# Constant products in TensorE's gaps at the handovers between the layers of a recurrent attention kernel

## The chip, the cores and the metric

The kernel runs on one core of a Trainium2 chip. The time is the device time of the core in microseconds; the number that counts is the median of several executions. A profile is one execution, recorded instruction by instruction by the hardware profiler.

## The reference, cut to what matters

Two kinds of layer alternate, A, B, A, B, each added to its input behind a layernorm. The input has 2048 tokens of width 512.

```python
# A: 64 segments of 32 tokens, one after the other, with 8 memory rows ahead of each
for s in range(n_seg):
    h = jnp.concatenate([mem, xs], axis=1)          # 40 rows
    q = jnp.einsum('btd,dhe->bhte', h, Wq)          # 32 heads of 128; k and v alike
    ...
    o = jnp.einsum('bhqk,bhke->bhqe', p, v)         # p: masked softmax
    o = jnp.einsum('bhte,hed->btd', o, Wo)
    mem = o[:, :M, :]                               # the next segment's memory
# B: linear attention over all tokens
kv = jnp.einsum('bhsd,bhse->bhde', pk, v)           # sums over every token
z = jnp.einsum('bhsd->bhd', pk)
o = num / den                                       # num = pq kv, den = pq z
x = x + o @ wo
```

Two things are serial by nature. A segment of A needs the memory rows of the segment before it. A token of B needs `kv` and `z` of all tokens, so no row of B can be finished before the last segment of A has run, and the second A can't start before the first tile of B is finished.

## The kernel before, in words

Weights stay in SBUF. The tokens are cut into 16 tiles of 128 rows (`NT`), a tile into four segments; `a_layer` loops over the 64 segments (`NSEG`). For a segment, the projections at L794 multiply the 40 rows by Wk, Wq and Wv (four products side by side in the array, each 32 columns wide). The results go through a transpose (L816, L842, or a DMA), scores (L937, L943), softmax, values (L980, L983, L1051), and then the output projection at L1085. The segment's output comes as two halves that L1110 (for the memory) or L1121 (for the tokens) adds up. The work of B is spread between the segments: `b_in` takes a finished tile of A through a layernorm (L753 to L759, transposed at L765), computes its keys and values (L1247), and adds the tile's part to `kva` (L1274) and `za` (L1276). `b_out` takes a tile back from DRAM as the second A layer needs it.

The handover from A through B to the next A is a single chain, for which no other work is left. In order:

- the last segment's output projection, L1085, its two copies on ScalarE (L623), and L1146, a product that puts the rows of the last segment into a tile; L1150 adds them to `x_sb`
- the layernorm of that last tile: L753, L754 on VectorE, L755, L757 on ScalarE, L759 on VectorE, the transpose L765 and its copy (L624)
- `b_in` of the last tile: keys and values by L1247 (4 products of 512 columns each), the function phi of the keys (L1231 on ScalarE, L1232 and L1234 on VectorE), the value copy (L623), `z` (L1265), `kv` (L1259), the queries (L1281), and the sums L1276 and L1274
- `b_mid`: the mask over the finished sums (L1295, L1299) and four products with the output weights, L1303, each copied back
- `b_out` of the first tile: L1350, its reciprocal as Ln and Exp on ScalarE (L1353, L1355), L1356, L1358 (4 products), and L1361, which adds the result to `x_sb`
- the layernorm of that tile for the second A layer, L753 to L765, the copies into `hT`, and the first projections, L794

After the second A and its `b_mid`, `b_out` runs over all 16 tiles instead, with nothing behind it; the tiles' inputs are loaded in large transfers by `last_rows`, while the last segments run.

The order of the work is not written out by hand. Each operation is a node of `_Prog` with its reads, writes, PSUM tiles and a cost from small formulas (`c_act`, `c_dve`, `c_pe`). `schedule` plays the engines in the planner's own time and picks, for each free engine, the ready node with the highest `prio`. A node's `prio` is the negative of its due time: `step * PERIOD + OFFSET[name][k]`, from a table with an entry for the k-th node of each named place. Nothing is picked ahead of a more urgent node that comes ready within `LOOK` (0.053 us). `finalize` then turns the edges (`sync`) into semaphore waits; an `order` edge only fixes the order on one engine. On the chip each engine runs its list in that order, whatever is ready behind. A PSUM tile is given one of 8 banks when its first node is placed.

One place already uses constant products: `warm` (L733 to L742) puts 14 products of `id_sb` and `Wq_sb` (L740) into the first segment, after its second scores.

Of the kernel before, what the change touches and what calls it, by code (L numbers as in the profile page):

```python
# [47 lines left out]
    "mem0F": (-317.25, -11.55, -397.30, -321.65, -320.25, -248.15, -253.70, -229.35, -133.00, -179.30),  # L48
    "mem1F": (-370.65, -140.65, -279.95, -318.75, -212.15, -221.80, -405.65, -341.75, -281.65, -211.10),
    "warm": (42.25,),  # L50
    "outF": (-402.35, -81.30, -402.15, -242.85, -347.15, -401.55, -307.80, -298.10, -276.25, -259.15),
    "nextF": (-375.70, -276.25, -244.45),
    "xF": (-98.95, -278.35, -377.95, -152.15, -135.25, 32.50, -346.60, -281.05, -333.80, -305.40, -12.30, -315.60,
# [49 lines left out]
def c_act(n, ptr=0, sb=0):  # L103
    return 0.17 + 0.833e-3 * n + 0.09 * ptr + 0.04 * sb


def c_dve(n, rate=1):
    return 0.155 + 1.044e-3 * n / rate
# [6 lines left out]
def c_pe(n_mm, n):  # L115
    return n_mm * max(0.0335, (n / 2.4 + 3.0) * 1e-3)
# [24 lines left out]
class _Prog:  # L141
# [27 lines left out]
    def add(self, engs, fn, cost, reads=(), writes=(), tiles=(), dsem=None, urgent=False, mode="full",  # L169
            after=(), lat=0.0):  # L170
        nd = _Node()
        nd.mode = mode
        nd.lat = lat
        nd.key = None
        if self.place is not None:
            step, name = self.place
            nd.key = (step, name, self.count)
            self.count += 1
        nd.soft = set()
        nd.engs = (engs,) if isinstance(engs, str) else tuple(engs)  # L180
        nd.cost = cost if isinstance(cost, dict) else {e: cost for e in nd.engs}
        nd.fn = fn
        nd.sync = set(after)
        nd.order = set()
        nd.tiles = tuple(tiles)
        nd.dsem = dsem
        nd.urgent = urgent
        nd.eng = nd.start = nd.done = nd.know = None
        nd.sig = False
        nd.val = 0  # L190
        nd.waits = []
        nd.idx = len(self.nodes)
        if dsem is not None:
            self.dma_tot[dsem] = self.dma_tot.get(dsem, 0) + 16
            nd.dval = self.dma_tot[dsem]
        for key in reads:
            st = self.res.setdefault(key, [None, []])
            if st[0] is not None:
                nd.sync.add(st[0])
            st[1].append(nd)  # L200
        for key in writes:
            st = self.res.setdefault(key, [None, []])
            if st[0] is not None and st[0] is not nd:
                nd.sync.add(st[0])
            for r in st[1]:
                if r is not nd:
                    nd.sync.add(r)
            st[0] = nd
            st[1] = []
        for tl in nd.tiles:  # L210
            if tl.ops:
                p = tl.ops[-1]
                if p.engs == ("pe",) and nd.engs == ("pe",):
                    nd.order.add(p)
                else:
                    nd.sync.add(p)
            tl.ops.append(nd)
        self.nodes.append(nd)
        return nd
# [270 lines left out]
def bass_interleave_layers__memory_aug_recurrent_mem_tr__linear_attn_block__prompt_kernel(  # L490
    nc: bass.Bass,
    A_x: bass.AP,
    A_mem0: bass.AP,
    A_Wq: bass.AP,
    A_Wk: bass.AP,
    A_Wv: bass.AP,
    A_Wo: bass.AP,
    A_seg_len: bass.AP,
    B_x: bass.AP,
    B_wqkv: bass.AP,  # L500
    B_wo: bass.AP,
    out: bass.AP,
):
    _build_kernel(nc, A_x, A_mem0, A_Wq, A_Wk, A_Wv, A_Wo, A_seg_len, B_wqkv, B_wo, out)


def _build_kernel(nc, A_x, A_mem0, A_Wq, A_Wk, A_Wv, A_Wo, A_seg_len, B_wqkv, B_wo, out):
# [8 lines left out]
    NSEG = S // SEG  # L516
# [14 lines left out]
    def sb(name, shape, dt=BF16):  # L531
        return E(nc.sbuf_tensor(name, shape, dt))
# [3 lines left out]
    Wv_sb = sb("Wv_sb", [128, 4, H * DH])  # L536
# [3 lines left out]
    id_sb = sb("id_sb", [128, 128])  # L540
# [76 lines left out]
    P = _Prog(nc, banks)  # L617
    add = P.add
# [19 lines left out]
    def x_move(o, i, k, reads, writes, kind, eng="pool", lat=2.0):  # L638
        add(eng, lambda e: e.dma_start(o, i), 0.55 if eng == "pool" else 0.4, reads=reads, writes=writes,  # L639
            dsem="%s%d" % (kind, k), lat=lat + (0.4 if eng == "pool" else 0.0))  # L640
# [3 lines left out]
    def slot(t):  # L644

        return (t + shift[0]) % NX
# [20 lines left out]
    def load_wo_b(n):  # L667
        add("pool", lambda e: e.dma_start(MB_sb[:, :, :], B_wo.rearrange("(c p) f -> p c f", p=128)), 1.1, after=[late[-1]],
            writes=[("MB", c) for c in range(4)], dsem="dwoB%d" % n, lat=4.0)
# [33 lines left out]
    for j in range(4):  # L703
# [15 lines left out]
    tl = P.tile()  # L719
    add("pe", lambda t, tl=tl: t.matmul(tl.f32()[:, 0:128], A8_sb[0:8, :], A8_sb[0:8, :], start=True, stop=True), 0.06,  # L720
        reads=XV, tiles=[tl])
    evac(maskbd_sb[:, :], lambda tl=tl: tl.f32()[:, 0:128], 128, tiles=[tl], writes=["maskbd"])
    tl = P.tile()
# [604 lines left out]
    def b_out(step, t, last):  # L1328

        P.at(step, ("boL" if t < NT - 1 else "boZ") if last else "bo" if t else "boF")  # L1330
        k = slot(t)
        x, xk = x_sb[:, k, :], ("x", k)
        e, ek, rb, rk = OWN if t else LEFT
        free = []
        if last:
            rb, rk = RE[:, t, :].bitcast(F32), [("RE", t)]
            free = P.res["Wk"][1]
            if t < NT - 1:
                e, ek, x, xk = XE[:, 0, t, :], [("XE", 0, t)], XE[:, 1, t, :], ("XE", 1, t)
            else:  # L1340
                e, ek = e_sb, ["e"]
        else:
            x_move(x, xs_view[t], k, [("xs", t)], [xk], "dxl")
            x_move(e, pq_view[t], k, [("pq", t)], ek, "dql" if t else "dq0")
        td, ty = P.tile(), P.tile()

        def md(pe):
            for c in range(4):
                o = slice(128 * c, 128 * c + 128)
                y = pe.matmul(td.f32()[:, o], zf_sb[:, c, :], e[:, o], start=True, stop=True)  # L1350
            return y
        add("pe", md, c_pe(4, 128), reads=["zf"] + ek, tiles=[td])
        add("act", lambda a: a.activation(rb, td.f32()[:, :], ACTF.Ln, bias=eps6_sb[:, 0:1]), c_act(512, 1),  # L1353
            reads=["eps6"], tiles=[td], writes=rk, after=free)
        add("act", lambda a: a.activation(rb, rb, ACTF.Exp, scale=-1.0), c_act(512, 0, 1), reads=rk, writes=rk)  # L1355
        add("dve", lambda v: v.tensor_tensor(e, e, rb, ALU.mult), c_dve(512), reads=ek + rk, writes=ek)  # L1356
        for c in range(4):
            add("pe", lambda pe, c=c: pe.matmul(ty.f32()[:, :], e[:, 128 * c:128 * c + 128], MB_sb[:, c, :],  # L1358
                                                start=(c == 0), stop=(c == 3)),
                c_pe(1, 512), reads=ek + [("MB", i) for i in range(4)], tiles=[ty])  # L1360
        add("dve", lambda v: v.tensor_tensor(x, x, ty.f32()[:, :], ALU.add), c_dve(512), reads=[xk], writes=[xk],  # L1361
            tiles=[ty])
        if last:
            x_move(o_view[t], x, t % 4, [xk], [], "dout", "sp")

    load_wo_b(1)
    a_layer(0, True)
    b_mid(NSEG + 2, 1)
# [5 lines left out]
    b_mid(2 * NSEG + 2, 3)  # L1374
    for t in range(NT):
        b_out(2 * NSEG + 2 + t, t, True)
    P.schedule()

    with nc.Block() as blk:
# [40 lines left out]
```

## Time and profile before

| | |
|---|---|
| Median of 5 runs | 1786.98 us (1782.03 to 1799.78) |
| The profiled execution: its own time | 1789.46 us |
| its span, from the first to the last instruction | 1787.3 us |
| TensorE busy in the span | 1665.1 us, 43,964 products |
| VectorE, ScalarE busy | 1061.6 us, 1172.0 us |
| Mean granted TensorE clock | 0.988 |
| PE busy in a stage inside the first layer (200 to 300 us) | 95.8 us of 100, clock 1.00 |
| PE busy in 870 to 880, 880 to 890, 890 to 900 us | 5.4, 5.5, 8.7 us of 10; clock 0.84, 0.84, 0.63 |
| PE busy in 1740 to 1750, 1750 to 1760 us | 7.4, 5.2 us of 10; clock 0.69, 0.67 |

The profile is read so: a row of the timeline gives the start, the time from the first start to the last end of a group of equal instructions, the engine, line and operation, and in brackets the idle time ahead of it with what ended it. The granted clock is a share of TensorE's full clock. The end of a product is modelled, about 0.2 us after its last column is issued, so that rows that follow each other overlap.

### The profile page before, as it was taken

The page shows a single profiled execution, that of the slowest core. Times are in us where ns is not written, and L with a number is a line of the kernel's source. Part 1 is how long each engine was busy: PE and PEld are TensorE (multiplying, and loading weights), DVE is VectorE, ACT ScalarE, POOL GpSimd, SP SyncE. Part 2 cuts the span into 40 slices and gives each one's busy share as a digit, 9 for nine tenths or more (in the row PEclk, how much of TensorE's full clock was granted, in tenths as well). Part 3 has the DMA queues.
Part 4 walks back from the last instruction along what each step waited for, and adds up shares of the span by engine and source line. Part 5 has one row for each costly group of instructions (what it writes and reads, how often), then busy time and mean ns, then how long its engine had stood idle before and what let it go on. Part 6 is the DMA issues. An engine that isn't in the chain of part 4 may idle for free.

```text
span 1787.3 us, 96722 instructions
## 1 busy us (share of the span) xinstructions
PE 1665.1 (93%) x43964; PEld 1068.6 (60%) x44043; DVE 1061.6 (59%) x3788; ACT 1172.0 (66%) x3117; POOL 326.3 (18%) x660
## 2 busy tenths in 40 slices
PE   5999999999999999999799999999999999999997
PEld 2656666665666665566455566656656656666563
DVE  3456666665666565565555566656655656665656
ACT  3666666666666666666466676767666766676665
POOL 2011212111221211222102111122211112221120
PEclk9999999999999999999899999999999999999998
DMA  9222323323233332332012333233333332332333
GB/s 377 78 48 53 57 53 53 58 51 56 50 57 53 54 58 47 56 56 51 21 34 44 56 56 64 46 59 59 55 57 56 52 57 53 59 57 53 61 77 98
DMA packets 295978, 113.46 MB, mean 63 GB/s; under 512 B 274552, under 2 KB 289712, under 8 KB 294032
## 3 DMA queue, kind: packets, MB, share of 16 engines
q1 hardware_dynamic: 272240, 74.91, 23.7%
q0 software_dynamic: 21744, 19.78, 5.4%
q10 hardware_dynamic: 1584, 12.58, 1.7%
q8 instruction: 344, 5.64, 1.4%
q14 instruction: 66, 0.54, 0.1%
HBM read 29.63 MB, written 10.49 MB: 22 GB/s over the span
## 4 chain that ended last, share of the span: by engine, by line
PE 63%; DMA 20%; DVE 9%; ACT 5%; issue 2%; POOL 1%; ACTq 0%; DVEq 0%
PE pb L794 31%; DMA arena_sb<-arena_sb 14%; PE pb L1085 12%; PE pb L1051 3%; PE pb L1247 3%; DVE arena_sb L624 3%; DMA dx_sb<-y_sb 2%; PE pb L816 2%; PE pb L970 2%; DMA arena_sb<-pq_scratch 2%; PE pb L937 1%; DMA Wk_sb<-in_A_Wk_dram 1%; ACT arena_sb L623 1%; PE pb L1281 1%; PE pb L1019 1%
## 5 line engine op out<-in xcount | busy, mean ns | idle before, releaser
L623 ACT ACTIVATE arena_sb<-pb 128x512 bf16<-128x512 f32 (+6 forms) x1433 | 709.7, 500 | 296.2 <-PE pb L794 187.2
L639 POOL DMA_DIRECT2D dx_sb<-y_sb x504 | 253.6, 509 | 1129.8 <-DVE arena_sb L624 659.5
L794 PE MATMUL pb<-Wv_sb,arena_sb 128*32 128x512 bf16 x5120 | 357.3, 379 | 2.6 <-issue 2.6
L794 PE MATMUL pb<-Wq_sb,arena_sb 128*32 128x512 bf16 x5120 | 347.4, 382 | 0.9 <-DMA Wq_sb<-in_A_Wq_dram 0.6
L1085 PE MATMUL pb<-Wo_sb,arena_sb 128*32 128x256 bf16 x10368 | 341.7, 276 | 6.8 <-DVE arena_sb L987 5.1
L794 PE MATMUL pb<-Wk_sb,arena_sb 128*32 128x512 bf16 x5120 | 343.9, 382 | 4.3 <-DMA Wk_sb<-in_A_Wk_dram 2.9
L1085 PEld LDWEIGHTS pb<-Wo_sb,arena_sb 128*32 128x32 bf16 x10368 | 264.6, 98 | 48.8 <-DVE arena_sb L987 12.9
L624 DVE COPY arena_sb<-arena_sb 128x128 bf16<-128x128 bf16 (+2 forms) x973 | 207.5, 213 | 143.4 <-DMA arena_sb<-arena_sb 89.0
L624 DVE COPY arena_sb<-pb 128x512 bf16<-128x512 bf16 (+2 forms) x311 | 117.9, 381 | 198.5 <-PE pb L816 177.6
L624 DVE CAST arena_sb<-pb 128x512 bf16<-128x512 f32 (+3 forms) x388 | 186.9, 488 | 43.6 <-PE pb L794 27.8
L794 PEld LDWEIGHTS pb<-Wk_sb,arena_sb 128*32 128x32 bf16 x5120 | 127.2, 97 | 129.5 <-DVE arena_sb L624 19.1
L794 PEld LDWEIGHTS pb<-Wq_sb,arena_sb 128*32 128x32 bf16 x5120 | 135.2, 98 | 115.4 <-issue 3.7
L623 ACT ACTIVATE outW_sb<-pb 128x128 fp32r<-128x128 f32 x290 | 80.3, 277 | 108.2 <-PE pb L1085 98.5
L794 PEld LDWEIGHTS pb<-Wv_sb,arena_sb 128*32 128x32 bf16 x5120 | 113.1, 95 | 59.2 <-issue 4.2
L954 ACT ACTIVATE arena_sb<-pb 128x192 bf16<-128x192 f32 (+1 forms) x256 | 84.0, 328 | 85.8 <-PE pb L937 84.1
L964 DVE TENSOR_TENSOR arena_sb<-arena_sb 128x128 bf16<-128x128 bf16 x504 | 90.6, 221 | 26.3 <-ACT arena_sb L954 22.3
L816 PEld LDWEIGHTS pb<-id_sb,arena_sb 128*32 128x32 bf16 x4320 | 82.1, 97 | 32.2 <-issue 1.4
L1051 PE MATMUL pb<-arena_sb 128*128 128x128 bf16 x1024 | 98.7, 221 | 1.5 <-DVE arena_sb L624 0.5
L816 PE MATMUL pb<-id_sb,arena_sb 128*32 128x128 bf16 x4320 | 97.1, 220 | 0.7 <-ACT arena_sb L623 0.7
L987 DVE TENSOR_TENSOR arena_sb<-pb,arena_sb 128x128 bf16<-128x128 f32 x252 | 68.8, 287 | 43.2 <-ACT arena_sb L975 31.2
L937 PE MATMUL pb<-arena_sb 128*32 128x40 bf16 x4096 | 69.1, 180 | 27.0 <-DMA arena_sb<-arena_sb 26.6
L1121 DVE TENSOR_TENSOR y_sb<-pb,outW_sb 64x256 bf16<-64x256 f32 x158 | 65.7, 416 | 44.3 <-ACT outW_sb L623 40.4
(122 smaller groups left out, 1966.9 us busy)
## 6 DMA issues: line engine op xcount, KB each, us to landing
arena_sb<-arena_sb SPq DMA_TRANSPOSE x480, 2.8
Wq_sb<-in_A_Wq_dram ACTq DMA_DIRECT2D x1, 4096.0 KB, 13.6
Wk_sb<-in_A_Wk_dram ACTq DMA_DIRECT2D x1, 4096.0 KB, 24.4
Wv_sb<-in_A_Wv_dram ACTq DMA_DIRECT2D x1, 4096.0 KB, 34.8
Wo_sb<-in_A_Wo_dram SPq DMA_DIRECT2D x4, 1024.0 KB, 11.7
xs_scratch<-x_sb POOLq DMA_DIRECT2D x32, 128.0 KB, 2.2
pq_scratch<-arena_sb POOLq DMA_DIRECT2D x32, 128.0 KB, 2.2
dx_sb<-y_sb POOLq DMA_DIRECT2D x252, 12.0 KB
```

What stands on the lines that cost most here:

```text
L623: return e.activation(o() if callable(o) else o, i() if callable(i) else i, ACTF.Copy)
L624: return e.tensor_copy(o() if callable(o) else o, i() if callable(i) else i)
L639: add(eng, lambda e: e.dma_start(o, i), 0.55 if eng == "pool" else 0.4, reads=reads, writes=writes, dsem="%s%d" % (kind, k), lat=lat + (0. ...
L794: r = pe.matmul(tl.f32()[32 * j:32 * j + 32, 0:512], blk[:, c, :], W[:, c, o:o + 512], start=(c == 0), stop=(c == 3), tile_position=(0, 32 ...
L816: r = pe.transpose(tt.bf16()[32 * j:32 * j + 32, 128 * i:128 * i + 128], img[:, k, o:o + 32], id_sb[:, :], tile_position=(0, 32 * j))
L937: r = pe.matmul(tl.f32()[32 * j:32 * j + 32, 40 * i:40 * i + 40], kT[:, hh, j, :], qT[:, hh, j, :], start=True, stop=True, tile_position=( ...
L954: add("act", lambda a: a.activation(PQ[:, r2, b, 0:nq], tl.f32()[:, 0:nq], ACTF.Exp, scale=SCALE), c_act(nq), tiles=[tl], writes=[("PQ", r ...
L964: add("dve", lambda v, a=a, p_=p_, w_=w_: v.tensor_tensor(wide(Pm[:, k, a, :]), p_.unsqueeze(2).to_broadcast([128, 4, 4, 8]), w_, ALU.mult ...
L987: add("dve", lambda v: v.tensor_tensor(oTb[:, s % NO, 16 * b:16 * b + 16, 0:8], pv.f32()[:, 0:128].rearrange("p (n q) -> p n q", q=8), Rm[ ...
L1051: r = pe.matmul(o, vimg[:, r2, e], Pbx[:, hh, :, :], start=i == 0, stop=False, skip_group_check=True)
L1085: r = pe.matmul(tl.f32()[32 * j:32 * j + 32, 0:256], oT[:, 4 * hh + n, :], Wo_sb[:, 8 * n + hh, 256 * d:256 * d + 256], start=(hh == 0 and ...
L1121: add("dve", lambda v: v.tensor_tensor(y_sb[0:64, k, :], tl.f32()[0:64, 0:256], outW[64:128, w, :].bitcast(F32), ALU.add), c_dve(256), rea ...
```

## The change

A function `keep_busy` is called after everything else has been put down and before `schedule`. It adds products of `id_sb` (128 x 128) and the first 256 columns of `Wv_sb` in 8 places; each place has one PSUM tile, which nobody reads. A place is tied by an `order` edge to one node of the chain, after which its products may stand, and the table gives all of them a due time 200 us behind their step, later than that of other work.

```diff
     "warm": (42.25,),
+    "fill": (200.00,),
...
+    FILL = (("outL", 7, 12), ("resL", 0, 24), ("biL", 5, 4), ("biL", 18, 8), ("biL", 27, 8), ("bm", 7, 21), ("boF", 9, 22),
+            ("prepF", 5, 4))
+
+    def keep_busy():
+
+        last = {n.key: n for n in P.nodes if n.engs == ("pe",) and n.key is not None}
+        for base in (0, NSEG):
+            for name, k, n in FILL:
+                step = base + NSEG + {"outL": 0, "resL": 0, "boF": -6, "prepF": -2}.get(name, 2)
+                node = last.get((step, name, k))
+                if node is None or (base and name == "bm"):
+                    continue
+                P.at(step, "fill")
+                tl = P.tile()
+                for i in range(n):
+                    P.count = 0
+                    nd = add("pe", lambda pe, tl=tl: pe.matmul(tl.f32()[:, 0:256], id_sb[:, :], Wv_sb[:, 0, 0:256], start=True,
+                                                               stop=True),
+                             c_pe(1, 256), reads=["id", "Wv"], tiles=[tl])
+                    if i == 0:
+                        nd.order.add(node)
+
...
         b_out(2 * NSEG + 2 + t, t, True)
+    keep_busy()
     P.schedule()
```

The third number of each entry is how many products stand at that place: 12 behind the last L1085, 24 behind L1146, 4 behind the transposes L765 of the last tile, 8 behind the values of L1247, 8 behind the queries L1281, 21 behind the second product of L1303, 22 behind the first tile's L1358, and 4 behind the transposes L765 of the next layer. As the planner places them, the 21 stand behind all four of L1303 and behind L1350. The first handover has all eight places (103 products). The second has the first five (56): the names of the last two don't occur there, and `bm` is left out by hand.

## Prediction

> **What bounds the kernel now.** I read the page first: its row of slices and its chain. Then I asked for the PE timeline around the two places where a layer pair ends, for the chain of waits there, and for stages of 1 us.
>
> ```profile
> PE   5999999999999999999799999999999999999997
> ...
> PEclk9999999999999999999899999999999999999998
> ...
> PE 63%; DMA 20%; DVE 9%; ACT 5%; issue 2%; POOL 1%; ACTq 0%; DVEq 0%
> ```
>
> TensorE is busy 93% of the span and carries 63% of the chain, so for most of the time the kernel is bound by products at full clock. Slices 20 and 40 are the exceptions: PE falls to 7 tenths and the clock to 8. These are the two handovers that the change touches. The PE timeline of the first one:
>
> ```profile
> 870.28 1.93 PE L1085 MATMUL pb<-Wo_sb,arena_sb 128*32 128x256 bf16 x64 [0.27 <-ACT arena_sb L623]
> 872.90 0.50 PE L1146 MATMUL pb<-outW_sb,selz_sb 128*128 128x256 f32 x2 [0.69 <-ACT outW_sb L623]
> 876.14 0.40 PE L765 MATMUL pb<-id_sb,arena_sb 128*128 128x128 bf16 x4 [2.74 <-DVE arena_sb L759]
> 877.46 3.05 PE L1247 MATMUL pb<-arena_sb 128*128 128x512 bf16 x7 [0.92 <-DVE arena_sb L624]
> ...
> 886.68 1.54 PE L1358 MATMUL pb<-arena_sb 128*128 128x512 bf16 x4 [2.27 <-DVE arena_sb L1356]
> 889.11 0.61 PE L1350 MATMUL pb<-arena_sb 128*128 128x128 bf16 x4 [0.89 <-DMA arena_sb<-pq_scratch]
> 890.96 0.61 PE L765 MATMUL pb<-id_sb,arena_sb 128*128 128x128 bf16 x4 [1.24 <-DVE arena_sb L759]
> 891.88 0.62 PE L794 MATMUL pb<-Wq_sb,arena_sb 128*32 128x512 bf16 x4 [0.32 <-DVE arena_sb L624]
> 892.29 0.64 PE L794 MATMUL pb<-Wv_sb,arena_sb 128*32 128x512 bf16 x4
> ```
>
> The brackets show PE standing between short products and waiting for VectorE and ScalarE. Two rows show its price: the same L765 takes 0.40 us at 876 and 0.61 at 890, and an L794 group follows the last after 0.41 us, where elsewhere in the layer it does after 0.216. (L1247 has 8 products; one record is missing, and the chain gives its place as 0.45 us of "issue" ahead of 877.46. I let it start at 877.03.) The clock by stages of 1 us (stage, length, PE busy, granted clock, DMA):
>
> ```profile
> 876.00:877.00 1.00, 0.40 (x4) 0.91 0.00 0
> 877.00:878.00 1.00, 0.54 (x2) 0.50 0.00 0
> ...
> 880.00:881.00 1.00, 0.77 (x6) 0.88 0.00 0
> ...
> 887.00:888.00 1.00, 1.00 (x4) 0.53 0.00 0
> ...
> 897.00:898.00 1.00, 1.00 (x20) 0.85 0.00 0
> ```
>
> A mean of 0.91 between 1 and 0.5 puts the change of clock at 876.82; in the same way 880.24, 887.06 and 897.30. The distances are 3.42, 6.82 and 10.24 us: 1, 2 and 3 times 3.41. So the clock is decided on a grid of 3.41 us. It falls after a window that is mostly idle (873.4 to 876.8, 12% busy by the stages, and 883.7 to 887.1, about a third), stays after one about 70% busy (880.2 to 883.7), and rises after one busy throughout (893.9 to 897.3). Mid-layer the clock also fell once behind an idle of only 1.67 us (at 682). The second handover has half clock from 1743.8 to 1750.6, behind a stall of 2.58 us that the change doesn't reach, and from 1754.0 to 1760.9.
>
> **The change part by part.** On all five engines the order stays as it was and each instruction waits for the same semaphores; PSUM banks are numbered differently. What is new is 159 products, 103 in the first handover and 56 in the second, each with its weight load. Nothing waits for them, they wait for nothing, no DMA and no other engine is touched. But PE works in order, so a block that is longer than its gap delays the chain's product behind it.
>
> Price of one. At full clock, 12 products of L1350 (128 columns) take 0.84 us and a single one 0.22, so (0.84-0.22)/11 = 0.056 a piece, weight load included; 4 of L1358 (512 columns) take 1.04 with 0.39 for one, 0.217 a piece. In between, 256 columns cost 0.110 us. At half clock it is half of L1247's 3.05/7 = 0.43, so 0.214. No row shows exactly this product; 0.110 and 0.214 are the two ends, and I take 0.110 because the fills themselves keep the windows busy.
>
> First handover, at 0.110, starting from where PE has issued the product before (about 0.17 us ahead of its modelled end):
> - 12 after L1085: 1.32 us from 872.03, to 873.35. L1146 was ready at 872.90: **0.45 late**.
> - 24 after L1146: 2.64 us, against a gap of about 2.9. Then 4 after L765 (0.44 against 0.66), 8 after L1247 (0.88 against 1.07), 21 after L1303 (2.31 against 2.42), 22 after L1358 (2.42 against 2.9), 4 after the second L765 (0.44 against 0.49): nothing late.
> - 8 after L1281: 0.88 against 0.83: **0.05 late**. L1350 of the next tile falls behind the 22 as well; its result isn't used until L1358 at 906, so I cost that at nothing. If its ScalarE work came into the way of the layernorm, it would cost up to one 0.69 us row.
>
> What full clock gives back there. L1247: keys are done after 4 x 0.43 and set Exp, VectorE and then L1265, 1.70 us from the start of Exp to L1265 in the rows; at full clock Exp starts 0.86 earlier in its stage, L1265 follows 1.70 later, and the values with their 0.60 copy are no longer last. L1259 comes at 880.40 instead of 881.20, with the 0.45 delay inside: **1.25 gained**. L1358: its end moves from 1.54 to about 1.04: **0.50**. L765: **0.21**. L794: 891.88 to 897.30 at half clock, PE without a gap, is half of 5.3: **2.63**. The sum is 4.6, less 0.5: 4.1 us. After 897 the layer is in the state in which it was before, only earlier. The next stop, 3.58 us of the tile's load at 907.41, is released by an L1358 in PE's order and moves along.
>
> Second handover. The clock is at half until 1750.6, so the 12 fills take about 1.6 us from 1750.12: L1146 is **0.68 late**. Gained are 0.21 on L765, 1.41 on L1247, 0.21 on L1259; 8 fills after L1281 cost 0.05. Net 1.1 us. From 1763 ScalarE is last (L1353 and L1355, 1.1 us a tile), at its own clock, and starts earlier by that much. Total: 4.1 + 1.1 = **5.2 us**.
>
> Bounds. Where the grid falls is the chance of each run. The L794 stretch costs 1.7 us (one window) to 3.4 (two), and a cold clock from L765 on would cost up to 0.9 more in L765, L1303 and L1358, and the second handover can have 1 us less; so the sum goes from 3.2 to 7.2. The profiled execution lies inside.
>
> Instruction fetch. The page gives 5.64 MB in 344 pieces, 16 KB each, for 96,722 instructions, so some 58 B for one; 318 more are 18 KB, about one piece. They shift where a piece ends in the second layer, and so where the 2.58 us stall beside the big loads at 1741.78 falls. I bound this by minus and plus 2.6 us and take nothing, since the loads and the rate of PE there are unchanged.
>
> A rule that speaks against the change: the Trainium skill, "TensorE: Matmul & The Clock Gate", section "Why this matters for your kernels", has the clock go down when PE idles for more than about 3 us between bursts, one whole window. The longest gap here is 2.74. By the rule there is nothing to prevent, and the fills only cost their delays, 0.45 + 0.05 + 0.68 + 0.05: 1.2 us slower. The rows show the clock at 0.50 behind gaps of 2.74 and 2.27 with short products around them, so I go by the row. The nearest row for the cure is in the first layer: where L740 runs 14 constant products in the gaps (34.28 to 38), the clock stays at 1.00 through stages that are 0.73 to 0.84 busy.
>
> **The rivals.**
> 1. *All of half clock's cost is on the path.* PE is busy for 3.2 and 8.1 us at half clock in the first handover and 5.7 in the second; half of that is 8.5. With no delays left, since gaps may be longer than their issue times let them seem, and with a worse grid in the runs of before (up to 2 more), it gives 8.5 to 10.5 us: about 1777. Against it: keys and values of L1247 lie partly beside the phi chain.
> 2. *The fills stand in front of the chain.* If they don't count as activity, or are granted half clock for another reason, each costs 0.214 and blocks overrun: 1.7, 2.2, 0.2, 1.5, 1.2, 2.0, 1.8 and 0.4 in order in the first handover, 10.9 together, and 6.8 in the second, 17.7 in all: **1804.7, slower**. The point is about 0.155 us a fill, where the overruns (7 us) eat the whole gain (6.4). Against it: the rate of products of this width at full clock, and L740.
> 3. *It does nothing*: the clock falls all the same at the first gap left, or the stall moves to the wrong side: -1 to +3 us, 1787 to 1788.
>
> **How the numbers follow.** The profiled execution took 1789.46 us (span 1787.3, and 2.2 around it), 2.5 above the median 1786.98. 5.2 less is 1784.3 for it; on the median, with 5.3 as the middle of 3.2 to 7.2, 1781.7. A measurement of this kernel can tell about 0.5% (8.9 us) from no change. Forecast: 0.64, of which 0.11 falls beyond 8.9 us, because the five times of before already span 18 us and a median of such moves by some 3. Rival 1: 0.17 (0.15 beyond). Rival 2: 0.12 (0.11 beyond). Rival 3: 0.07 (0.01 slower). That makes 0.26 faster, 0.62 the same, 0.12 slower. The range 1774 to 1792 takes in the forecast, rival 3 and most of rival 1, and leaves out most of rival 2.
>
> **What would show it.** Right: clock 1.00 from 870 to 900, and from 1751 to the end; L765 at 0.40 both times; L1247's 8 products in 1.75 us; L794 groups 0.216 apart from the start; the step from the first L1085's end to L1146 0.45 us longer. The stretch from the last L1085 to the first L794 of the second layer, 19.7 us now, would take about 18.2. Wrong: fills 0.21 apart, or L765 waiting for PE and not for L759, or a clock of 0.50 inside the fills, or a new wait further into the second layer that takes the gain back.

## The result and the profile after

The changed kernel took **1780.13 us** (median of 27 runs, 1774.22 to 1785.72) beside 1785.72 us for the kernel before (46 runs): a ratio of **0.9965 [0.9953, 0.9977]**, 6.3 us less (the ratio is that of the means; the medians are 5.6 apart). Run again in a later session (below) it gave 0.9948 [0.9933, 0.9963]. The prediction was 1781.7 on a median of 1786.98, a ratio of 0.9970. The profiled execution took 1779.78 us, with a span of 1777.6. In the changed kernel every line above the new code stands one further down (L1085 is now L1086), and the new products are L1383.

The page of the changed kernel, the three rows that answer to those of before:

```profile
PE   5999999999999999999999999999999999999997
...
PEclk9999999999999999999999999999999999999999
...
PE 65%; DMA 19%; DVE 8%; ACT 5%; issue 2%; POOL 1%; ACTq 0%; DVEq 0%
```

Both dips, in slice 20 and slice 40, are gone from the clock, and slice 20 is gone from the busy row. (A busy PE at the handovers now says nothing of work: most of it is L1383.) The chain's shares hardly move (PE 65%, 63 before): what was removed is a few us in 1780.

The PE timeline of the first handover in the changed kernel; "x12" is the number of products in the group, and a row without a bracket had no idle time worth a mention ahead of it:

```profile
868.88 1.93 PE L1086 MATMUL pb<-Wo_sb,arena_sb 128*32 128x256 bf16 x64 [0.28 <-ACT arena_sb L624]
870.75 1.49 PE L1383 MATMUL pb<-Wv_sb,id_sb 128*128 128x256 bf16 x12
871.99 0.48 PE L1147 MATMUL pb<-outW_sb,selz_sb 128*128 128x256 f32 x2
872.31 2.79 PE L1383 MATMUL pb<-Wv_sb,id_sb 128*128 128x256 bf16 x24
875.21 0.40 PE L766 MATMUL pb<-id_sb,arena_sb 128*128 128x128 bf16 x4
...
876.35 1.67 PE L1248 MATMUL pb<-arena_sb 128*128 128x512 bf16 x7 [0.31 <-DVE arena_sb L625]
...
884.59 1.04 PE L1359 MATMUL pb<-arena_sb 128*128 128x512 bf16 x4
...
888.37 0.40 PE L766 MATMUL pb<-id_sb,arena_sb 128*128 128x128 bf16 x4
...
889.13 0.40 PE L795 MATMUL pb<-Wq_sb,arena_sb 128*32 128x512 bf16 x4
889.36 0.39 PE L795 MATMUL pb<-Wv_sb,arena_sb 128*32 128x512 bf16 x4
```

The gaps of 2.74 and 2.27 us are filled, L766 takes 0.40 us both times (0.61 at the second before), L1248 1.67 for the recorded 7 (3.05), L1359 1.04 (1.54), and the L795 groups follow after 0.22 us. The visible price is that L1147 starts behind the block of 12 instead of by itself, 0.49 us later, and L1304 behind the block of 8, 0.09 us later. The stages of the changed kernel over the same place (start, length, PE, PEld, DVE, ACT and POOL busy, granted clock, DMA):

```profile
870.00:880.00 10.00, 9.58 (x115) 7.30 (x105) 4.58 (x11) 2.25 (x6) 1.11 (x2) 1.00 0.10 28
880.00:890.00 10.00, 9.83 (x96) 7.16 (x98) 7.09 (x19) 4.91 (x10) 1.08 (x2) 1.00 0.09 28
890.00:900.00 10.00, 10.00 (x273) 5.73 (x269) 3.80 (x9) 5.82 (x12) 0.00 (x0) 1.00 0.01 3
```

The clock is 1.00 throughout, where it was 0.84, 0.84 and 0.63.

The second handover went otherwise in this execution. Its PE rows, and the VectorE rows of the same time:

```profile
1738.36 2.79 PE L1383 MATMUL pb<-Wv_sb,id_sb 128*128 128x256 bf16 x24
1745.05 0.61 PE L766 MATMUL pb<-id_sb,arena_sb 128*128 128x128 bf16 x4 [3.90 <-DVE arena_sb L760]
```

```profile
1741.82 0.42 DVE L1163 TENSOR_TENSOR x_sb<-x_sb,dx_sb 96x512 bf16<-96x512 bf16 x1 [6.67 <-DMA dx_sb<-y_sb]
1742.35 0.69 DVE L1151 TENSOR_TENSOR x_sb<-x_sb,pb 128x512 bf16<-128x512 bf16 x1
```

The 24 products ended at 1741, and then PE stood for 3.90 us more (L766 came 7.01 us after L1147; before it was 3.24) and the clock fell again (0.50 from 1745 to 1748). What was late is a small transfer: L1163 adds the rows of the last tile's earlier segments, its DMA was issued at 1733.78 beside the large loads for the end, and it landed only at 1741.8. L1151, for which L1147 had made the product in time, stands behind L1163 on VectorE.

### The profile page after: what moved, and what is told of

Same layout as the page of the kernel before. It is cut to its first block, busy times and chain, and to the rows that moved or that the text cites. A ratio compares the mean times of both kernels' runs of the same rounds, so it can differ in the third digit from the quotient of the medians.

```text
span 1777.6 us, 97038 instructions
## 1 busy us (share of the span) xinstructions
PE 1666.6 (94%) x44121; PEld 1076.7 (61%) x44202; DVE 1062.1 (60%) x3788; ACT 1173.1 (66%) x3117; POOL 326.4 (18%) x660
## 4 chain that ended last, share of the span: by engine, by line
PE 65%; DMA 19%; DVE 8%; ACT 5%; issue 2%; POOL 1%; ACTq 0%; DVEq 0%
PE pb L795 33%; DMA arena_sb<-arena_sb 15%; PE pb L1086 11%; PE pb L1052 3%; PE pb L1248 3%; DVE arena_sb L625 2%; DMA dx_sb<-y_sb 2%; PE pb L971 2%; PE pb L817 2%; PE pb L938 2%; DMA Wk_sb<-in_A_Wk_dram 1%; PE pb L1282 1%; ACT arena_sb L624 1%; PE pb L1020 1%; PE pb L1111 1%
## 5 line engine op out<-in xcount | busy, mean ns | idle before, releaser
L795 PE MATMUL pb<-Wv_sb,arena_sb 128*32 128x512 bf16 x5120 | 356.6, 378 | 0.1
L795 PE MATMUL pb<-Wk_sb,arena_sb 128*32 128x512 bf16 x5120 | 343.8, 382 | 4.7 <-DMA Wk_sb<-in_A_Wk_dram 4.3
L795 PE MATMUL pb<-Wq_sb,arena_sb 128*32 128x512 bf16 x5120 | 345.1, 380 | 0.6 <-DMA Wq_sb<-in_A_Wq_dram 0.6
L1086 PE MATMUL pb<-Wo_sb,arena_sb 128*32 128x256 bf16 x10368 | 335.5, 273 | 5.6 <-DVE arena_sb L988 3.7
L1086 PEld LDWEIGHTS pb<-Wo_sb,arena_sb 128*32 128x32 bf16 x10368 | 260.9, 97 | 45.4 <-DVE arena_sb L988 11.3
L795 PEld LDWEIGHTS pb<-Wk_sb,arena_sb 128*32 128x32 bf16 x5120 | 127.3, 97 | 129.9 <-DVE arena_sb L625 18.4
L795 PEld LDWEIGHTS pb<-Wq_sb,arena_sb 128*32 128x32 bf16 x5120 | 134.8, 97 | 113.7 <-issue 1.6
L795 PEld LDWEIGHTS pb<-Wv_sb,arena_sb 128*32 128x32 bf16 x5120 | 112.9, 95 | 56.3 <-issue 0.8
L938 PEld LDWEIGHTS pb<-arena_sb 128*32 128x32 bf16 x4096 | 51.0, 94 | 65.1 <-DMA arena_sb<-arena_sb 48.5
```

The costliest lines, as they stand in the source:

```text
L795: r = pe.matmul(tl.f32()[32 * j:32 * j + 32, 0:512], blk[:, c, :], W[:, c, o:o + 512], start=(c == 0), stop=(c == 3), tile_position=(0, 32 ...
L938: r = pe.matmul(tl.f32()[32 * j:32 * j + 32, 40 * i:40 * i + 40], kT[:, hh, j, :], qT[:, hh, j, :], start=True, stop=True, tile_position=( ...
L1086: r = pe.matmul(tl.f32()[32 * j:32 * j + 32, 0:256], oT[:, 4 * hh + n, :], Wo_sb[:, 8 * n + hh, 256 * d:256 * d + 256], start=(hh == 0 and ...
```

## The experiments

All ratios are against the kernel before on the same chip in the same session. Two stretches are read from each profile. **H1** goes from the end of the last L1085 of the first layer to the first L816 of the second layer: 26.88 us before, 22.87 after. **H2** goes from the last L1015 row, 4 to 9 us ahead of the last L1085 of the second layer, to the first L1303 behind it: 22.63 us before, 21.72 after. H2 starts earlier because the PE stops beside the large loads fall on one side of the last L1085 or on the other.

**One handover alone.**

```diff
-        for base in (0, NSEG):
+        for base in (0,):          # first handover only
+        for base in (NSEG,):       # second handover only, in the other kernel
```

> The constant products stand only in the first handover (103); the second is as before. My theory (full clock is the gain, 4 us of it in the first handover; in the second the rows of the last tile wait for their transfers behind the large loads, so its fills bring about 1 us or nothing): the stretch from the last L1085 of the first layer to the first L816 of the second takes 22.9 us as with all fills, against 26.9 before; half clock comes back in the second handover; the time is 0 to 2 us above the changed kernel, ratio to before about 0.997. Rival (the second handover brings a good part of the 6 us): the time is 3 us or more above the changed kernel, ratio about 0.9985.

> The 56 products of the second handover alone. My theory (the second handover waits for the transfers of its last rows, so that full clock brings little there): first stretch as before, 26 to 28 us; time 0 to 2 us below before, ratio 0.999 to 1.000. Rival (the second handover brings a third of the whole or more): 2.5 us or more, ratio 0.9985 or less.

The first handover alone took 1775.92 us (22 runs; before 1780.30 in 61): **0.9972 [0.9957, 0.9987]**, 5.0 us less, H1 22.87, H2 20.76. So most of the change is here, and it is as large as forecast. The second alone took 1773.27 (before 1775.68): 0.9984 [0.9965, 1.0004], 2.8 us less, H1 26.47, H2 20.65. Its interval holds both expectations, and its middle lies on the side of the rival (2.5 us or more), so the run does not decide between them.

The mean clock that every run lists is a steadier witness than the time. Lost clock, (1 - clock) x span, is 15.9 us on the mean of the 61 runs of before, 8.9 with the first handover filled and 6.6 in the 27 runs of the whole change; with the second alone it is 12.6, beside 15.0 in its own session. The first handover's products thus save 7.1 us of lost clock and the second's 2.5. Together that is 9.6. For the whole change it is 9.3 across two sessions, and 11.2 in the later session that has both (16.1 to 5.0, with only 5 runs of the change). Not all of it is on the path.

**What must the products be?** Three kernels change one product's form or number.

```diff
-    pe.matmul(tl.f32()[:, 0:256], id_sb[:, :], Wv_sb[:, 0, 0:256], ...)
+    pe.matmul(tl.f32()[:, 0:8], id_sb[:, :], Wv_sb[:, 0, 0:8], ...)                       # thin
+    pe.matmul(tl.f32()[0:32, 0:256], id_sb[:, 0:32], Wv_sb[:, 0, 0:256], ...,
+              tile_position=(0, 0))                                                       # narrow
...
-                for i in range(n):
+                for i in range(n // 2):                                                   # half
```

> All 159 products stay in their places, with their weight loads, but stream 8 columns instead of 256. My theory (what counts is the time in which columns stream through the array): the clock falls to 0.5 in the first handover as before, the stretch from the last L1085 to the first L816 takes 26 to 28 us, and the time is that of before within 2 us, ratio 0.999 to 1.001. Rival (any instructions on TensorE will do, or the gain is a matter of where the instruction stream is cut): the clock stays at 1.00, the stretch takes 22.4 us and the ratio is 0.9965 or a little less.

> The same 159 products of 256 columns, but with 32 columns of weights instead of 128, so a quarter of the array. My theory (the time in which columns stream counts, not the share of the array): the clock stays at 1.00, the first stretch takes 22.9 us, ratio 0.9965. Rival (the share of the array counts): the clock falls in the first handover and blocks of half clock stand in front of the chain, the stretch takes 30 us or more, ratio over 1.002.

> Half as many products in every block: 6, 12, 2, 4, 4, 10, 11, 2. They end in the gaps without delaying anything, and leave about half of each gap idle. Before, the clock fell after windows of 3.41 us that were 51% busy or less and stayed after one that was 70% busy; here the windows are 50 to 75% busy, depending on where the grid falls. My theory (a window needs between 51 and 70%): in most executions one window of the first handover fails, the stretch from the last L1085 to the first L816 takes 24 to 26 us, ratio 0.998 to 0.999. Rival (any products spread through the gap are enough): clock at 1.00, stretch 22.4 us, ratio 0.996.

*Thin* keeps all 159 products and their weight loads, but each streams 8 columns: 0.9990 [0.9974, 1.0006], H1 26.15, H2 21.99, lost clock 14.9. Its PE timeline of the first handover:

```profile
866.71 0.76 PE L1383 MATMUL pb<-Wv_sb,id_sb 128*128 128x8 bf16 x24
869.61 0.61 PE L766 MATMUL pb<-id_sb,arena_sb 128*128 128x128 bf16 x4 [2.14 <-DVE arena_sb L760]
870.01 0.29 PE L1383 MATMUL pb<-Wv_sb,id_sb 128*128 128x8 bf16 x4
870.73 3.60 PE L1248 MATMUL pb<-arena_sb 128*128 128x512 bf16 x8 [0.43 <-DVE arena_sb L625]
```

The 24 products are over in 0.76 us, the gap stays open for 2.14, and L766 (0.61 us) and L1248 run at half clock. The number of instructions buys nothing; the time streamed does. *Narrow* streams the same 256 columns through 32 columns of weights: 0.9959 [0.9942, 0.9976], H1 23.16, clock 1.00. So the share of the array in use doesn't count either. The 0.29 us more than 22.87 lie at changes between narrow and full products: the block of 24 starts 0.43 us after L1147 (0.32 in the change), L766's follow-up 0.32 after it (0.23). Its H2, 21.95, has a wait of 3.95 us like the change's own.

*Half* has 6, 12, 2, 4, 4, 10, 11 and 2 products. I had expected the clock to fall in places and H1 to get worse; that did not happen. It took 1772.12 us, 0.9957 [0.9941, 0.9974], with H1 at 22.38, and the gaps that it leaves do not cost anything:

```profile
872.10 0.40 PE L766 MATMUL pb<-id_sb,arena_sb 128*128 128x128 bf16 x4 [1.41 <-DVE arena_sb L760]
...
881.48 1.04 PE L1359 MATMUL pb<-arena_sb 128*128 128x512 bf16 x4 [1.18 <-DVE arena_sb L1357]
...
885.25 0.40 PE L766 MATMUL pb<-id_sb,arena_sb 128*128 128x128 bf16 x4 [0.91 <-DVE arena_sb L760]
```

L766 and L1359 run at full clock behind 1.41 and 1.18 us of idle. From 868 to 890 PE is busy for 17.1 of 22 us (78%); the emptiest stretch of 3.41 us, from 870.0, for 1.7 (50%). But that stretch is not one of the windows of the clock. The 100 changes of clock that the 14 profiles show between 20 and 1766 us lie, in each profile, on one grid of 3.413 us, all to within 0.03 us. So the changes elsewhere in a profile tell where the windows fall at its handover. In *half* the emptiest window there begins at 871.21 and is 65% busy. The first row below is that window; the other two are windows of the kernel before after which the clock fell, and the one at 678.86 lies in the middle of a layer (49% busy; its longest gap is the last row):

```profile
871.21:874.62 3.41, 2.23 (x14) 1.12 (x15) 0.84 (x2) 0.88 (x3) 0.55 (x1) 1.00 0.20 71
```

```profile
678.86:682.27 3.41, 1.68 (x39) 1.13 (x39) 1.49 (x8) 1.48 (x6) 0.55 (x1) 1.00 0.00 0
883.66:887.07 3.41, 1.14 (x9) 0.57 (x8) 2.45 (x4) 2.21 (x4) 0.83 (x2) 1.00 0.11 38
```

```profile
680.74 0.28 PE L937 MATMUL pb<-arena_sb 128*32 128x40 bf16 x16 [1.67 <-DMA arena_sb<-arena_sb]
```

Cut along these grids, every window of the 14 profiles between 40 and 1762 us has a clock of 1.00 or 0.50 from end to end. Of those at 1.00, 36 were followed by half clock, and none of these was more than 55.5% busy; some 6,970 were not, and none of these was less than 46% busy. In between both occurred. (A few records of products can be missing from a profile, so the shares are not exact.) Half the products thus stay above the limit, with 65% here and 57% in half-spread (below), but not by much: a grid with a window on the 50% stretch would put them inside the band. The runs give no sign that this happens often: lost clock is 5.0 us in the mean of the 5 runs of half and 4.1 in the 12 of half-spread, beside 5.0 in the change's own 5.

**The price of one product, and of the delays.**

```diff
-    FILL = (("outL", 7, 12), ... ("biL", 27, 8), ...            # as changed
+    FILL = (("outL", 7, 7), ... ("biL", 27, 7), ...             # trim
...
+                    def two(pe, tl=tl):                         # twice: each node issues its product twice
+                        for d in range(2):
+                            r = pe.matmul(tl.f32()[:, 0:256], id_sb[:, :], Wv_sb[:, 0, 0:256], ...)
```

> The block behind the last L1085 has 7 products instead of 12 and the block behind L1281 7 instead of 8, in both handovers, so that no block is longer than its gap. My theory (a block that is too long delays the chain by its excess): L1146 follows 0.69 us behind the last L1085 as before the change, not 1.18; the clock stays at 1.00; the stretch from the last L1085 to the first L816 takes 22.4 us instead of 22.9; the second handover hides the same behind the loads, so 0.5 to 1 us in all, ratio about 0.996. Rival (the clock needs the whole block): half clock in the first handover, 23 us or more.

> Each of the 159 places issues its product twice, at unchanged order, so that nearly every block is longer than its gap. By the price of 0.110 us the excess over the changed kernel in the first handover is 1.3, 2.4, 0.2, 0.7, 0.9, 2.2, 1.9 and 0.4 us in order, 10.1 in all: the stretch from the last L1085 to the first L816 takes 33 us. In the second the first blocks hide behind the large loads and 1.8 remain. Time about 12 us above the changed kernel, ratio to before about 1.0033. Rival (a fill costs more than 0.110 once it stands in the way, 0.155 say): the stretch takes 41 us, and the ratio is over 1.009.

*Trim* shortens the two blocks that were forecast to be too long. L1147 starts 0.69 us after L1086 again, H1 is 22.44 us, 0.43 less than the change and as worked out, and the clock stays at 1.00; 0.9976 [0.9960, 0.9991]. *Twice* puts 318 products in the same places, with the order of the rest unchanged: 1.0069 [1.0041, 1.0098], H1 32.89. Its PE timeline:

```profile
871.08 5.41 PE L1386 MATMUL pb<-Wv_sb,id_sb 128*128 128x256 bf16 x48
876.33 0.39 PE L766 MATMUL pb<-id_sb,arena_sb 128*128 128x128 bf16 x4
```

L766 has no bracket left: it waits for PE, not for L760. The 48 take 5.41 us with some 0.2 of modelled end, so 0.108 to 0.110 a piece, also when they stand in the way and the clock is 1.00. H1 came out at the 33 of the sum by 0.110; by 0.214 it would have been 41. The ratio lies between the two expectations: the total came out higher than my own by some 6 us, of which H2 (23.28, 1.6 above the change) is a part; the rest lies in the scatter between the handovers, and I can't place it.

**The change and the kernel before, again.**

> The changed kernel once more, as a second profiled execution and for the comparison with the others here. First handover 22.9 us from the last L1085 to the first L816, within 0.1, since its clock and its blocks are the same; ratio to before about 0.9965. The second handover and the stretch between the two vary from execution to execution (836 to 848 us so far for the stretch).

> The kernel before, unchanged, for a second profiled execution. What I want to see is how much its first handover varies with where the grid of the clock falls: the stretch from the last L1085 to the first L816 was 26.9 us in the first profile and 26.2 in the kernel with thin products, which comes near to it. My theory (the rest of the 6 us is the mean over the grid): 25.5 to 28.5 us, different from 26.9. Rival (it is always 26.9, and the gain beyond 4 us comes from somewhere else): 26.9 within 0.2.

> The kernel before once more, a third profiled execution. The same two expectations: a stretch of 25.5 to 28.5 us that differs from execution to execution, or 26.9 within 0.2 each time.

The change gave 1770.73 us beside 1780.52, 0.9948 [0.9933, 0.9963], H1 22.86 and H2 19.47. Two more profiles of the kernel before have H1 26.82 and 26.18. Over all profiles without products in the first handover, H1 is 26.88, 26.82, 26.18 and 26.47 (and 26.15 with the thin ones); with them it is 22.87, 22.87 and 22.86. So the gain of 4.0 in the first pair of profiles is 3.7 on the mean (26.59 - 22.87), and it is the filled side that is the same each time. I had expected other positions of the grid to cost the kernel before more than 26.88 us; in none of these profiles they do, so they don't explain a gain beyond 4 us. H2 varies on both sides: 22.63, 21.48, 21.73 and 20.76 without products, mean 21.65; 21.72, 19.47, 20.65 and 18.94 (trim) with them, mean 20.20. That is 1.5 us apart, with a spread of about 2 to 3 within each kind; with the thin kernel (21.99) on the one side and narrow (21.95) and half (20.62) on the other, it is 1.2.

**The loads beside the second handover.**

```diff
-                    after=P.res["Wq"][1], dsem=...
+                    after=P.res["Wq"][1] + [m for m in P.nodes if i and m.key == (step, "resL", 1)], dsem=...
```

The second to fourth group of the large loads wait for L1150, so that only the first runs beside the last tile's small transfers. It stands once with the trimmed blocks (spread) and once with half the products (half-spread).

> The trimmed blocks (7 and 7), and in addition the second to fourth group of the large loads for the last layer wait for L1150 of the last tile; order and waits of the other engines are the same. My theory (the second handover waits for its last rows because their small transfers are behind 3.9 MB of loads): the stretch from the last L1085 to the first L1303 takes 9.7 us there, against 11.2 to 15.6 in the kernels with fills so far, L1085 has no stop inside, L1162 is no longer what comes last, and the tiles of the last layer don't wait for their loads, which have 5 us and more; 3 to 5 us below the trimmed kernel, ratio to before about 0.994. Rival (the loads are needed early, or TensorE's stop has another cause): the gain comes back as waits of L1350 for the loads, ratio 0.9965 or more.

> Half of every block, and the later groups of the large loads wait for L1150 of the last tile. If half the products are enough for the clock, as they were in one profile, the first stretch takes 22.4 us and the second (last L1085 to first L1303) about 10.8, bound by the issue of the last rows' transfers; 0.5 to 2 us below the changed kernel, ratio about 0.995. If they are enough only for some places of the grid, the first stretch takes 23.5 us or more.

*Spread*: H2 falls to 17.09 us, without a PE stop (from the end of the last L1085 to L1303 it is 10.87 us, where 9.7 was expected), but L1163 still waits:

```profile
1733.07 0.42 DVE L1163 TENSOR_TENSOR x_sb<-x_sb,dx_sb 96x512 bf16<-96x512 bf16 x1 [3.26 <-DMA dx_sb<-y_sb]
```

```profile
1728.26 2.02 POOL L640 DMA_DIRECT2D dx_sb<-y_sb  x4 [0.78 <-issue]
```

The second row, of POOL, gives a part of the reason: it issues the small transfers one after another, some 0.5 us each, so the third, with which L1163's wait ends on the chain, is out only at 1729.77. It then took 3.20 us to land; in the changed kernel it took 6.44. The expected 0.994 was not reached: 1772.16 us, 0.9951 [0.9935, 0.9968], no better than the change on the same chip, although H2 is 2.4 us shorter than in that profile. *Half-spread* confirmed that half the products hold the clock (H1 22.38, clock 1.00); it has the best median of its session, 1768.25 us beside 1775.68, but at 0.9952 [0.9934, 0.9971] it can't be told from the change. From the last L1085 to L1303 it takes 9.78 us (10.8 expected). In its profile L1163 waits for only 0.38 us, and yet PE stops:

```profile
1730.35 1.14 PE L1086 MATMUL pb<-Wo_sb,arena_sb 128*32 128x256 bf16 x33 [2.66 <-issue]
```

The stop begins at 1727.7, just as the first load ends, and from 1728 to 1730 the DMA queues move only 4 to 8 GB/s. So holding back the later loads does not prevent the stop, and that the loads' traffic causes it is not shown.

## Why the prediction was right

The mechanism and the size were right: 5.2 us forecast, 6.3 [4.1, 8.4] measured and 9.3 [6.6, 11.9] in the second session, intervals that overlap. By its own steps, for the profiled pair:

| Step in the first handover | forecast | measured |
|---|---|---|
| L1085's end to L1146, behind the 12 | +0.45 | +0.49 (0.69 to 1.18) |
| L765 to L1259, with L1247 at full clock | -1.25 | -1.25 (5.06 to 3.81) |
| L1259 to L1303, behind 8 after L1281 | +0.05 | +0.09 (1.95 to 2.04) |
| L1358 to the second L765 | -0.50 | -0.50 (4.28 to 3.78) |
| second L765 to the first L794 | -0.21 | -0.16 (0.92 to 0.76) |
| first L794 to the first L816 | -2.63 | -2.66 (7.21 to 4.55) |
| sum | -4.1 | -4.0 (26.88 to 22.87) |

The stretches left out, L1146 to L765 and L1303 to L1358, changed by 0.02 us and nothing. From the last L1085's end to the first L794 it is 18.32 us, where 18.2 was forecast. Nothing further into the second layer took the gain back: the first handover alone is 5.0 [2.3, 7.7] us faster.

**The price.** 0.110 us was taken from 128- and 512-column products; the rows and the doubled kernel give the same. **The delays.** Both that the first handover was charged with are real, and taking them away gives 0.43 back in H1; L1350 behind the 22 cost nothing, as assumed.

**The rule against it.** The Trainium skill, "TensorE: Matmul & The Clock Gate", section "Why this matters for your kernels", would have made the change 1.2 us slower, since no gap is above 3 us. The measured clock sides with the row: in all four profiles of the first handover without products it fell, with no gap above 2.83 us, and it held where they were filled. Counted from the last column issued, some 0.2 us ahead of the modelled end, the longest gaps do come to about 3 us. But the clock also fell at 887.07 behind 2.27 us and in the middle of a layer behind 1.67. What goes with it in all 14 profiles is how busy the window of 3.413 us was: below about half.

**Rival 1** (all half-clock cost on the path, 8.5 us or more) has a number that the second session would bear out. But it asks for 5.7 in the first handover, half of the forecast's 3.2 and 8.1 us, and the rows give 4.0. (Cut at the changes of clock, PE is busy there for 2.8 and 7.8 us at half clock, so rival 1 asks for 5.3.) With nothing delayed, in *half*, they give 4.5. **Rival 2** (products in front of the chain at 0.214) fell with the clock of 1.00 and with the doubled kernel: 32.89 us and not 41. **Rival 3** fell with the 4.0. The thin kernel, with H1 at 26.15 and half clock, is what rival 3 would have looked like.

**What was weak.** The second handover's term, 1.1 us, was worked out from one profile as if its stall always came at the same place. It doesn't. Beside the large loads PE stops for 1.2 to 2.7 us ("issue") at a different product each time, ahead of the last L1085, inside it, or not at all, and the transfer that L1163 waits for comes late. The wait of L765 was taken as 2.74 us; the two later profiles of before have 3.88 and 3.64 there. In the changed kernel's own profile the stop ahead of L1085 was gone, L766 still waited for 3.90 us behind the 24 products, and the clock fell, because their block was sized for a gap of 2.9. The averages (1.2 to 1.5 us in H2, 2.5 us of lost clock, 2.8 [-0.7, 6.2] us of time) agree with 1.1, but none of them measures it well, so that this term came out near is in part luck. Instruction fetch, which I took as nothing between minus and plus 2.6, can't be separated from this. What stays open is where the measured time beyond H1 and H2 comes from, and how much of it is real. The two add up to some 5 us (3.7 and 1.2 to 1.5); that lies inside the first session's interval and below the second's. The runs of before span 25 us and those of the change 11.5, and the stretch from the first L816 to the start of the last L1085 of the second layer alone differs by up to 11 us between profiles (837 to 848).

## What to carry to other kernels

Where short products of a serial chain leave TensorE mostly idle, look at the granted clock behind the gaps, and price the half clock by what of it lies on the chain: here 10.6 us of PE at half clock were worth 4. Constant products in the gaps buy that back at their streaming time, so they must be long in time rather than many, and each block shorter than its gap; half-filled gaps served as well as full ones here and leave the chain no delay, as long as every window of the clock stays well above half busy. Where large transfers run beside the chain, settle which wait ends last first: there the block is sized for a gap that isn't the same in the next run.

## What was not expected of the hardware

- Neither the longest gap nor an average over the handover tells whether the clock falls; the busy share of the one window of 3.413 us on its grid does, all but a band from 46% to 55%. Half the products hold the clock with PE idle for up to 1.41 us at a time, since their windows are at least 65% busy; mid-layer the clock fell behind a window that was 49% busy, with no gap above 1.67 us. The way back is a different matter: windows at half clock had to be at least 73% busy before the clock rose, and up to 82% was not always enough.
- Outside the handovers, and apart from the start and the end, the clock fell now and then for one window, in some executions and not in others of the same kernel: four times in the profile of before, not in one of its two repeats and once in the other, once in the change's repeat. No product of the change is near.
- Going from products of 128 weight columns to products of 32 cost about 0.1 us each time (the narrow kernel: 0.43 us instead of 0.32, 0.32 instead of 0.23).
- Doubling the constant products, 159 more of them, left the clock at 1.00 and their price at 0.110 us: 32 us of nearly unbroken streaming brought no throttle.
